# A fused attention and feed-forward kernel: 32-column matmuls written to the four row quarters of a PSUM bank

## The chip, the cores and the metric

The kernel runs on one core of one Trainium2 chip. The metric is the device time of one execution in microseconds (us), less is better. The core's engines are TensorE (PE; its weight loads are listed apart as PEld), VectorE (DVE), ScalarE (ACT), GpSimd (POOL) and SyncE (SP, which here issues all DMAs). Each engine works its own instructions off in order and waits for others by semaphores.

## The reference

An attention through 32 inducing points, then a feed-forward block whose activation is a rational function, over 4 batches of 12480 rows of 128 numbers:

```python
def mab(q, kv):
    s = scale * (q @ kv.transpose(0, 2, 1))
    s = s - s.max(-1, keepdims=True)
    a = np.exp(s)
    a /= a.sum(-1, keepdims=True) + 1e-09
    return a @ kv
h = mab(I, x)            # 32 inducing rows attend to all 12480 rows: "pooling"
y = mab(x, h)            # every row attends to the 32 pooled rows

h1 = y @ w_in            # 128 -> 2048
P = a[0] + a[1] * h1 + a[2] * h1**2 + a[3] * h1**3
Q = 1.0 + abs(b[0]) * abs(h1) + abs(b[1]) * h1**2
out = (P / (Q + 1e-06)) @ w_out      # 2048 -> 128
```

## The kernel before, in words

Rows of x are taken in blocks of 480 (4 chunks of 120), 26 blocks a batch. The main work is the feed-forward block. A unit is one block and two of the sixteen 128-column pieces of w_in; there are 4 x 26 x 8 = 832 units, and `fast_ticks` (line 887) advances by one unit a step. In a step PE computes h of the next unit (`first`, tiles hp, f16), adds a shift (`moved`, hp from by and same) and multiplies the unit of 13 steps ago by w_out (`second`, two fp32 matmuls of 128x128 by 128x480 into po); DVE makes the instructions u<-hp, l<-u,all,hp and l<-l,all,u, ACT takes Abs, a logarithm and a sigmoid, POOL two instructions every second step.

Beside it, the attention of the batches is worked off by two generators, `ahead` (the pooling of the next batch) and `attend` (the rows' own attention). They yield what their next piece needs ("pe", "v" for DVE, "wait") with a cost; `side` (line 782) adds a gain a step to each account (`SPARE`, line 195: 0.75 for "pe", kept up to 2.5, at most 1.7 spent in a step) and lets a generator go on as far as the account covers. So the yields' costs set how the side work is spread over the steps. All of it is written in program order on each engine.

Two pieces of `ahead` concern us:

- `pass1` (line 372), the scores of the inducing points. Four blocks make a group; 26 blocks are six groups of four and one of two. Tile pc holds 128 rows, 32 for each of the four blocks. The stationary operand is a 128-column window of ind, which is 224 columns wide, zero but for the 32 inducing points in its middle, so that block j adds to rows 32 j to 32 j + 31 and adds zero elsewhere; the group's matmuls accumulate into one bank. DVE then copies pc to e and takes the maxima. Each matmul yields 0.8 (line 384).
- `pooled` (line 444), the weighted sums. After Exp on ACT, PE transposes a group of e (tile pt), ACT copies it to eT, and 16 matmuls (4 blocks j, 4 chunks c) of 120x32 by 120x129 all accumulate into rows 0 to 31 of tile ph (line 485); the 129th column of x is one and sums the weights. Each yields 0.2. DVE adds ph to the accumulator acc (32 rows). At the end of the batch acc gives rs and H, and HT is H transposed.

The operands come by DMA: x_c blocks as tiles xTa (pass1) and x_t blocks as tiles x (pooled), in four buffers each; the next block's load is written when the one before is taken, and POOL sets the column of ones of x. Batch 0's pass1 and pooled run before the main work, in `before` (line 976), with loads of four or three blocks at a time (xTw, xw), while the loads of the weights (raw) are slipped in between; DVE and POOL then convert the weights from 64-bit floats (cv), and `main` starts.

One PSUM bank, misc, is shared by all side matmuls (`misc`, line 218).

Of the kernel before, what the change touches and what calls it, by code (L numbers as in the profile page):

```python
# [9 lines left out]
F32 = mybir.dt.float32  # L10
# [6 lines left out]
ALU = mybir.AluOpType  # L17
PSUM = bass.MemoryType.PSUM

P = 128  # L20
TP = 120
M = 32
C = 128
HB = 4
BT = HB * TP
# [167 lines left out]
class Kernel:  # L193
# [78 lines left out]

    def setup(self):
        nc, cp = self.nc, self.cp
        self.ind = cp.tile([C, 7 * M], F32, name="ind")
        nc.vector.memset(self.ind, 0.0)
        nc.sync.dma_start(out=self.ind[:, 3 * M:4 * M], in_=self.ind_c)
        self.ident = cp.tile([P, P], F32, name="ident")
        make_identity(self.tc.nc, self.ident)
        self.ones = cp.tile([1, 4], F32, name="ones")  # L280
        nc.vector.memset(self.ones, 1.0)
        self.ident4 = cp.tile([M, 4, M], F32, name="ident4")
        for j in range(4):
            nc.vector.tensor_copy(out=self.ident4[:, j], in_=self.ident[0:M, 0:M])
        self.many = cp.tile([M, 4], F32, name="many")
        nc.vector.memset(self.many, 1.0)
        self.w_max = cp.tile([C, 8], F32, name="w_max")
        self.w_in = cp.tile([C, self.F], F32, name="w_in")
        self.w_out = cp.tile([P, self.NF, C], F32, name="w_out")
# [82 lines left out]
    def pass1(self, b):  # L372

        nc, ap = self.nc, self.ap
        X = mybir.AxisListType.X
        e = ap.tile([P, self.NG, BT], F32, tag="e", name=f"e{b}")
        mxs = ap.tile([P, self.NG, 2], F32, tag="mxs", name=f"mxs{b}")
        nc.gpsimd.memset(mxs, -3.0e38)
        xs = self.wide_columns(b) if self.boot else self.cols.pop((b, "a"))
        for g in range(self.NG):  # L380
            nb = min(4, self.NB - 4 * g)
            yield from self.landed("a", b, g)
            for j in range(nb):
                yield "pe", 0.8
                if j == 0:
                    pc = self.misc(f"pc{b}_{g}")
                nc.tensor.matmul(pc[:, 0:BT], self.ind[:, M * (3 - j):M * (7 - j)], next(xs), start=(j == 0), stop=(j == nb - 1))
            rows = slice(0, M * nb)
            for i in range(2):
                yield "v", 0.36  # L390
                c = slice(BT // 2 * i, BT // 2 * (i + 1))
                nc.vector.tensor_scalar(out=e[rows, g, c], in0=pc[rows, c], scalar1=1.0, scalar2=None, op0=ALU.mult, op1=ALU.max, accum_out=mxs[rows, g, i:i + 1])
            self.free()
        if self.boot:
            self.wide_rows(b)
        else:
            self.xs[b] = [self.x_rows(b, n) for n in range(4)]
        yield "v", 0.1
        mx = ap.tile([P, 1], F32, tag="mx", name=f"mx{b}")
        nc.vector.tensor_reduce(out=mx, in_=mxs.rearrange("p g i -> p (g i)"), axis=X, op=ALU.max)  # L400
        yield "pe", 0.2
        pm = self.misc(f"pm{b}")
        nc.tensor.transpose(out=pm[0:1, 0:P], in_=mx, identity=self.ident)
        yield "v", 0.3
        mt = ap.tile([1, 1, M], F32, tag="mt", name=f"mt{b}")
        nc.vector.tensor_reduce(out=mt[:, 0], in_=pm[0:1, 0:P].rearrange("o (j m) -> o m j", m=M), axis=X, op=ALU.max)
        self.free()
        nm = ap.tile([1, 4, M], F32, tag="H", name=f"nm{b}")
        nc.vector.tensor_scalar(out=nm, in0=mt.broadcast_to((1, 4, M)), scalar1=-1.0 / math.sqrt(C), scalar2=None, op0=ALU.mult)
        yield "pe", 0.2  # L410
        pb = self.misc(f"pb{b}")
        nc.tensor.matmul(pb[:, 0:4], nm.rearrange("o j m -> o (j m)"), self.ones, start=True, stop=True)
        yield "v", 0.1
        nmc = ap.tile([P, 1], F32, tag="nmc", name=f"nmc{b}")
        nc.vector.tensor_copy(out=nmc, in_=pb[:, 0:1])
        self.free()
        self.e[b] = e
        self.exps.append(lambda: self.exp_rows(b, e, nmc))
        self.flush()
# [24 lines left out]
    def pooled(self, b, own=None):  # L444

        nc, ap = self.nc, self.ap
        e = self.e[b]
        acc = ap.tile([M, C + 1], F32, tag="acc", name=f"acc{b}")
        xs = self.xs.pop(b)

        def turned(g):
            rows = slice(0, M * min(4, self.NB - 4 * g))
            for c in range(HB):
                yield "pe", 0.22
                if c == 0:
                    pt = self.misc(f"pt{b}_{g}").rearrange("p (c n) -> p c n", c=HB)
                nc.tensor.transpose(out=pt[0:TP, c, rows], in_=e[rows, g, TP * c:TP * c + TP], identity=self.ident[rows, rows])
            eT = ap.tile([TP, HB, P], F32, tag="eT", name=f"eT{b}_{g}", bufs=2)
            yield from self.act(lambda: nc.scalar.activation(eT[:, :, rows], pt[0:TP, :, rows], AF.Identity, bias=0.0, scale=1.0))
            eTs.append(eT)  # L460

        eTs, early = [], int(self.boot)
        while self.e_done.get(b, 0) < self.NG:
            self.flush()
            yield "wait", 0
        if early:
            yield from turned(0)
        for g in range(self.NG):
            nb = min(4, self.NB - 4 * g)
            if g + early < self.NG:  # L470
                yield from turned(g + early)
            eT = eTs.pop(0)
            self.free()
            yield from self.landed("x", b, g)
            for k in range(HB * nb):
                j, c = divmod(k, HB)
                yield "pe", 0.2
                if k == 0:
                    ph = self.misc(f"ph{b}_{g}")
                if c == 0 and self.boot and (4 * g + j) % 3 == 0 and g + j:  # L480
                    self.xs[b] = xs
                    self.wide_rows(b)
                elif c == 0 and not self.boot and 0 < 4 * g + j < self.NB - 3:
                    xs.append(self.x_rows(b, 4 * g + j + 3))
                nc.tensor.matmul(ph[0:M, 0:C + 1], eT[:, c, M * j:M * j + M], xs[4 * g + j][:, c, :], start=(k == 0), stop=(k == HB * nb - 1))
            yield "v", 0.2
            if g == 0:
                nc.vector.tensor_copy(out=acc, in_=ph[0:M, 0:C + 1])
            else:
                nc.vector.tensor_tensor(out=acc, in0=ph[0:M, 0:C + 1], in1=acc, op=ALU.add)  # L490
            self.free()
        yield "v", 0.2
        rs = ap.tile([M, 1], F32, tag="rs", name=f"rs{b}")
        nc.vector.tensor_scalar(out=rs, in0=acc[:, C:], scalar1=1e-9, scalar2=None, op0=ALU.add)
        nc.vector.reciprocal(out=rs, in_=rs)
        yield "v", 0.2
        H = ap.tile([M, C], F32, tag="H", name=f"H{b}")
        nc.vector.tensor_scalar(out=H, in0=acc[:, 0:C], scalar1=rs, scalar2=None, op0=ALU.mult)
        yield "pe", 0.3
        pt = self.misc(f"HT{b}")  # L500
        nc.tensor.matmul(pt[:, 0:4 * M], H, self.ident4.rearrange("p a m -> p (a m)"), start=True, stop=True)
        yield "v", 0.2
        while own is None and self.scored < b - 2:
            yield "wait", 0
        HT = own if own is not None else ap.tile([C, 4 * M], F32, tag="HT", name=f"HT{b}", bufs=2)
        nc.vector.tensor_copy(out=HT, in_=pt[:, 0:4 * M])
        self.free()
        self.HT[b] = HT
# [436 lines left out]
    def last_on_pool(self, d, before):  # L945

        G, p = self.nc.gpsimd, self.params
        if d:
            G.tensor_scalar(out=before.u, in0=d.g, scalar1=1.0, scalar2=p.z_k3, op0=ALU.mult, op1=ALU.add)
            G.tensor_tensor(out=d.g, in0=before.u, in1=d.u, op=ALU.mult)  # L950
# [25 lines left out]
    def before(self):  # L976

        nc = self.nc
# [4 lines left out]
        self.setup()  # L983
        loads, words = self.weights(), []
        for n, _ in enumerate(self.pass1(0)):
            if n >= 36 and n % 6 == 3:
                words += [w for w in [next(loads, None)] if w]
        self.params = Params(self.tc.nc, self.cp, self.moe_a, self.moe_b)
        for n, _ in enumerate(self.pooled(0, self.cp.tile([C, 4 * M], F32, name="HT0"))):
            if n % 20 == 5:  # L990
                words += [w for w in [next(loads, None)] if w]
        words += list(loads)
        self.params.derive()
# [106 lines left out]
```

## Time and profile before

| what | value |
|---|---|
| time, median of 3 runs | 2593.8 us (2586.8 to 2594.12) |
| the profiled execution, its own time | 2591.88 us |
| its span, first to last instruction | 2589.7 us |
| mean granted TensorE clock | 0.974 |
| busy: PE, DVE, ACT, POOL | 92%, 88%, 83%, 56% of the span |

How to read it: a busy share is an average over the whole span; the main work begins some 115 us into it, and from about 1800 us on `ahead` has nothing left to do. What a piece of work costs is read from stretches of equal numbers of steps. Matmul records overlap in the trace (a record's length holds its latency), so the pace is taken from starts, not lengths. An fp32 matmul shows as two weight loads and two matmul records. All instructions of the main work bear line 177, that of a helper; they are told apart by their tiles.

### The profile page before, as it was taken

Reading aid. Unit: us, or ns where it says so; the run is one execution under the profiler, and the core shown is the slowest. Engines: PE = TensorE matmul, PEld = TensorE weight load, DVE = VectorE, ACT = ScalarE, POOL = GpSimd, SP = SyncE. Lnnn points to the kernel's source line nnn. Section 1 sums busy time; section 2 is a strip of 40 time slices with the busy share of each in tenths; the row PEclk is TensorE's granted clock in tenths of the full one; section 3 lists DMA queues with packets and bytes.
Section 4 is the critical chain, followed back from the end, with each engine's and each line's share of the span. In section 5 each row is a group of like instructions: output and inputs, shape, how many; then the busy total and the mean of one; then the engine's idle time right before and its main releaser. Section 6 shows DMA issues by size and latency. Waiting matters only on the chain.

```text
span 2589.7 us, 25944 instructions
## 1 busy us (share of the span) xinstructions
PE 2376.2 (92%) x8662; PEld 1206.7 (47%) x8662; DVE 2267.1 (88%) x2487; ACT 2151.0 (83%) x1487; POOL 1448.1 (56%) x997
## 2 busy tenths in 40 slices
PE   8589998999989999899999999999999999999997
PEld 5344544455544444455544444554444444444443
DVE  2698899878998899888899889888999999999996
ACT  1178789978887889988888789887889899899996
POOL 0335456555655565555655555555656566666666
PEclk9679999999999999999999999999999999999999
DMA  9112210021011310121121210221010101000000
GB/s 241 60 31 72 83 52 12 27 69 50 27 54 53 88 54 16 35 62 50 31 62 54 81 40 25 62 58 38 20 45 18 44 16 33 14 23 20 16 16 17
DMA packets 117112, 121.03 MB, mean 47 GB/s; under 512 B 13289, under 2 KB 115561, under 8 KB 116969
## 3 DMA queue, kind: packets, MB, share of 16 engines
q1 hardware_dynamic: 116969, 119.28, 16.3%
q8 instruction: 70, 1.15, 0.2%
q14 instruction: 73, 0.60, 0.1%
HBM read 80.89 MB, written 25.56 MB: 41 GB/s over the span
## 4 chain that ended last, share of the span: by engine, by line
PE 50%; DVE 28%; issue 8%; ACT 7%; POOL 2%; DMA 1%; SPq 1%; DVEq 0%; POOLq 0%; ACTq 0%
PE po L177 29%; DVE l L177 12%; DVE u L177 11%; PE hp L177 11%; ACT u L177 5%; PE pd L177 3%; PE ph L177 3%; PE pc L177 2%; DVE oT L177 1%; ACT L177 1%; POOL l L177 1%; DVE asm L177 1%; POOL u L177 1%; SPq L177 1%; PE pl L177 1%
## 5 line engine op out<-in xcount | busy, mean ns | idle before, releaser
L177 PE MATMUL po<-l,w_out 128*128 128x480 f32 x3328 | 1568.2, 575 | 10.6 <-POOL l L177 8.4
L177 DVE SCALAR_TENSOR_TENSOR l<-u,all,hp 128x960 f32<-128x960 f32 x832 | 1001.8, 1204 | 44.8 <-PE hp L177 29.9
L177 POOL TENSOR_SCALAR u<-l,all 128x960 f32<-128x960 f32 x416 | 446.2, 1073 | 945.6 <-DVE l L177 796.5
L177 POOL TENSOR_TENSOR l<-u 128x960 f32<-128x960 f32 x416 | 927.7, 2230 | 34.6
L177 PEld LDWEIGHTS po<-l,w_out 128*128 128x128 f32 x3328 | 624.3, 192 | 372.3 <-issue 209.2
L177 ACT ACTIVATE u<-u,all 128x1920 f32<-128x1920 f32 x416 | 765.6, 1887 | 1.2
L177 ACT ACTIVATE u<-u 128x1920 f32<-128x1920 f32 x416 | 737.5, 1797 | 3.0 <-DVE l L177 1.8
L177 DVE TENSOR_SCALAR u<-hp 128x960 int32<-128x960 int32 x520 | 597.2, 1148 | 125.1 <-PE hp L177 118.3
L177 ACT ACTIVATE u<-hp,all 128x960 f32<-128x960 f32 x312 | 328.2, 1052 | 289.8 <-PE hp L177 289.1
L177 DVE SCALAR_TENSOR_TENSOR l<-l,all,u 128x960 f32<-128x960 f32 x416 | 523.9, 1260 | 2.4 <-ACT u L177 2.4
L177 PE MATMUL hp<-at,st 128*128 128x480 f16 x1664 | 477.5, 369 | 20.4 <-DVE l L177 17.9
L177 PE MATMUL hp<-same,by 96*128 96x480 f16 x1040 | 301.3, 371 | 129.9 <-DVE u L177 124.6
L177 PEld LDWEIGHTS <-st 128*128 128x128 f16 x1872 | 182.6, 98 | 483.8 <-issue 468.7
L177 ACT ACT_TABLE_LOAD x235 | 301.5, 1283 | 4.7 <-PEq L1093 0.7
L177 PEld LDWEIGHTS <-by 96*128 96x128 f16 x1040 | 102.3, 98 | 356.7 <-issue 319.4
L177 DVE COPY oT<-po 128x480 f32<-128x480 f32 x104 | 67.8, 652 | 68.9 <-PE po L177 68.4
L177 PEld LDWEIGHTS pd<-HT,xTb 128*120 128x120 f32 x832 | 104.9, 200 | 16.4 <-issue 8.9
L177 PE MATMUL pd<-HT,xTb 128*120 128x32 f32 x832 | 101.8, 278 | 2.9 <-DMA xTb<-x_c 2.6
L177 PE MATMUL ph<-x,eT 120*32 120x129 f32 x624 | 76.7, 274 | 1.6 <-DMA x<-x_t 1.6
L177 PEld LDWEIGHTS ph<-x,eT 120*32 120x32 f32 x624 | 65.0, 109 | 22.6 <-issue 14.8
L177 PE MATMUL pc<-xTa,ind 128*128 128x480 f32 x156 | 71.9, 566 | 1.0 <-DMA xTa<-x_c 1.0
L177 PE MATMUL po<-at,st 128*128 128x480 f16 x208 | 59.1, 366 | 0.0
(108 smaller groups left out, 666.9 us busy)
## 6 DMA issues: line engine op xcount, KB each, us to landing
xTb<-x_c SPq DMA_DIRECT2D x104, 240.0 KB, 2.8
out<-oT SPq DMA_DIRECT2D x104, 240.0 KB, 2.0
xTa<-x_c SPq DMA_DIRECT2D x78, 240.0 KB, 2.7
x<-x_t SPq DMA_DIRECT2D x78, 240.0 KB, 3.4
at<-hl SPq DMA_DIRECT2D x416, 30.0 KB, 1.8
xw<-x_t SPq DMA_DIRECT2D x8, 720.0 KB, 13.6
xTw<-x_c SPq DMA_DIRECT2D x5, 960.0 KB, 11.9
raw<-w_in SPq DMA_DIRECT2D x4, 480.0 KB, 12.3
```

What stands on the lines that cost most here:

```text
L177: ins = call(*args, **kw)
```

## The change

Both kinds of matmul use a 32-column stationary operand and write 32 rows of the bank at a quarter's offset. In `pass1` ind is the inducing points alone, and block j of a group writes rows 32 j to 32 j + 31 in a matmul of its own, with no accumulation. In `pooled` chunk c writes quarter c, accumulated over the blocks j, so ph and acc have 128 rows; a new constant fold (four identities of 32 under each other) sums the quarters by one matmul per batch (pq), from which rs and H are made. The yields become 1.0 for a group in pass1 and 0.4 for four matmuls in pooled, and the weights' loads in `before` are placed by other counts, since there are fewer yields.

```diff
-        self.ind = cp.tile([C, 7 * M], F32, name="ind")
-        nc.vector.memset(self.ind, 0.0)
-        nc.sync.dma_start(out=self.ind[:, 3 * M:4 * M], in_=self.ind_c)
+        self.ind = cp.tile([C, M], F32, name="ind")
+        nc.sync.dma_start(out=self.ind, in_=self.ind_c)
...
+        self.fold = cp.tile([P, M], F32, name="fold")
+        for j in range(4):
+            rows = slice(M * j, M * j + M)
+            nc.vector.tensor_copy(out=self.fold[rows], in_=self.ident[rows, rows])
...
+            yield "pe", 1.0
+            pc = self.misc(f"pc{b}_{g}")
             for j in range(nb):
-                yield "pe", 0.8
-                if j == 0:
-                    pc = self.misc(f"pc{b}_{g}")
-                nc.tensor.matmul(pc[:, 0:BT], self.ind[:, M * (3 - j):M * (7 - j)], next(xs), start=(j == 0), stop=(j == nb - 1))
+                nc.tensor.matmul(pc[M * j:M * j + M, 0:BT], self.ind, next(xs), start=True, stop=True)
...
-        acc = ap.tile([M, C + 1], F32, tag="acc", name=f"acc{b}")
+        acc = ap.tile([P, C + 1], F32, tag="acc", name=f"acc{b}")
...
-                yield "pe", 0.2
+                if c == 0:
+                    yield "pe", 0.4
...
-                nc.tensor.matmul(ph[0:M, 0:C + 1], eT[:, c, M * j:M * j + M], xs[4 * g + j][:, c, :], start=(k == 0), stop=(k == HB * nb - 1))
+                nc.tensor.matmul(ph[M * c:M * c + M, 0:C + 1], eT[:, c, M * j:M * j + M], xs[4 * g + j][:, c, :], start=(j == 0), stop=(j == nb - 1))
             yield "v", 0.2
             if g == 0:
-                nc.vector.tensor_copy(out=acc, in_=ph[0:M, 0:C + 1])
+                nc.vector.tensor_copy(out=acc, in_=ph[:, 0:C + 1])
             else:
-                nc.vector.tensor_tensor(out=acc, in0=ph[0:M, 0:C + 1], in1=acc, op=ALU.add)
+                nc.vector.tensor_tensor(out=acc, in0=ph[:, 0:C + 1], in1=acc, op=ALU.add)
             self.free()
-        yield "v", 0.2
+        yield "pe", 0.3
+        pq = self.misc(f"pq{b}")
+        nc.tensor.matmul(pq[0:M, 0:C + 1], self.fold, acc, start=True, stop=True)
+        yield "v", 0.4
...
-        nc.vector.tensor_scalar(out=H, in0=acc[:, 0:C], scalar1=rs, scalar2=None, op0=ALU.mult)
+        nc.vector.tensor_scalar(out=H, in0=pq[0:M, 0:C], scalar1=rs, scalar2=None, op0=ALU.mult)
+        self.free()
...
-            if n >= 36 and n % 6 == 3:
+            if n >= 18 and n % 3 == 1:
...
-            if n % 20 == 5:
+            if n % 8 == 5:
```

The change also moves instructions, since the yields' costs set the places. On PE, the second group of batch 1's scores (pc_1; po, hp are the main work, st and by its f16 weights, xTa_n the blocks of x), before:

```order
L177 MATMUL pc_1_1274<-xTa_4_1198,ind 128x480
L177 MATMUL pc_1_1274<-xTa_5_1229,ind 128x480
L177 MATMUL po_2_0_1245<-l_2_3_1040,w_out 128x480
L177 LDWEIGHTS st_612
L177 MATMUL hp_4_2_1282<-at_1_0_1110,st_612 128x480
L177 LDWEIGHTS st_612
L177 MATMUL hp_4_2_1282<-at_1_0_1110,st_612 128x480
L177 MATMUL po_2_0_1245<-l_2_3_1040,w_out 128x480
L177 MATMUL pc_1_1274<-xTa_6_1242,ind 128x480
```

and now:

```order
L177 MATMUL hp_4_0_1256<-same,by 128x480
L177 MATMUL pc_1_1280<-xTa_4_1204,ind 32x480
L177 MATMUL pc_1_1280<-xTa_5_1207,ind 32x480
L177 MATMUL pc_1_1280<-xTa_6_1210,ind 32x480
L177 MATMUL pc_1_1280<-xTa_7_1281,ind 32x480
L177 MATMUL po_2_0_1252<-l_2_3_1046,w_out 128x480
```

A group of four stood on three steps (its fourth matmul follows one step later) and stands on one; over batches 1 to 3 the 78 pc matmuls stood on 54 steps and stand on 21, often two steps apart.

On PE, the first group of batch 1's pooling (ph_0; "x4" is one block's four chunks), the second half of it before:

```order
L177 MATMUL po_14_0_2820<-l_14_6_2711,w_out 128x480
L177 LDWEIGHTS by
L177 MATMUL hp_16_4_2880<-same,by 128x480
L177 MATMUL ph_0_2891<-x_2_2021,eT_0_2768 32x129 x4
L177 MATMUL ph_0_2891<-x_3_2024,eT_0_2768 32x129 x4
L177 MATMUL po_14_0_2820<-l_14_7_2721,w_out 128x480
```

and the whole group now:

```order
L177 MATMUL hp_12_6_2466<-same,by 128x480
L177 MATMUL ph_0_2496<-x_0_1569,eT_0_2452 32x129 x4
L177 MATMUL ph_0_2496<-x_1_1572,eT_0_2452 32x129 x4
L177 MATMUL ph_0_2496<-x_2_1575,eT_0_2452 32x129 x4
L177 MATMUL ph_0_2496<-x_3_1578,eT_0_2452 32x129 x4
L177 MATMUL po_11_0_2522<-l_11_0_2286,w_out 128x480 x2
```

The two halves of a group stood on two steps that follow each other (13 steps a batch, 39 in all) and now stand on one (7 a batch, 21 in all), the next group five or more steps later. The group stands some 30 steps earlier in the program than before.

On DVE, at the end of batch 0's pooling, before the main work (acc takes up the last group, ph_6; cv are the conversions of the weights), now:

```order
L177 SCALAR_TENSOR_TENSOR cv_515<-raw_180,cv_515 128x480
L177 TENSOR_TENSOR acc_214<-ph_6_392,acc_214 128x129
L77 TENSOR_TENSOR all<-all 128x1
L177 TENSOR_SCALAR cv_523<-raw_189 128x480
L146 CAST flag<-all 128x1
L177 TENSOR_SCALAR rs_406<-pq_404 32x1
```

The last accumulation stands inside the first of the eleven conversions (cv_515); before, it stood behind four whole ones and the start of two more.

## Rows read from the trace of the kernel before

**Rows 1.** The page: span, engines' busy time, POOL's two groups of the main work.

```profile
span 2589.7 us, 25944 instructions
PE 2376.2 (92%) x8662; PEld 1206.7 (47%) x8662; DVE 2267.1 (88%) x2487; ACT 2151.0 (83%) x1487; POOL 1448.1 (56%) x997
...
L177 POOL TENSOR_SCALAR u<-l,all 128x960 f32<-128x960 f32 x416 | 446.2, 1073 | 945.6 <-DVE l L177 796.5
L177 POOL TENSOR_TENSOR l<-u 128x960 f32<-128x960 f32 x416 | 927.7, 2230 | 34.6
```

**Rows 2.** Busy time in three stretches of 16 steps: scores, pooling, neither.

```profile
core 0: us, PE busy (x) PEld busy (x) DVE busy (x) ACT busy (x) POOL busy (x), PEclk, DMA share, GB/s
1439.20:1489.10 49.90, 47.95 (x147) 22.45 (x146) 45.25 (x54) 42.47 (x29) 27.34 (x17) 1.00 0.25 70
1630.50:1681.40 50.90, 49.07 (x213) 26.87 (x213) 41.39 (x43) 42.59 (x32) 28.93 (x26) 1.00 0.22 60
2396.40:2436.30 39.90, 37.77 (x121) 17.58 (x120) 39.55 (x38) 39.38 (x27) 26.37 (x16) 1.00 0.06 19
```

**Rows 3.** Groups of these three stretches: count, busy us, mean ns, idle us before.

```profile
L177 DVE SCALAR_TENSOR_TENSOR l<-u,all,hp 128x960 f32<-128x960 f32 x17 | 20.5, 1204 | 0.6 <-PE hp L177 0.6
L177 PE MATMUL pc<-xTa,ind 128*128 128x480 f32 x24 | 11.1, 565 | 0.0
...
L177 DVE SCALAR_TENSOR_TENSOR l<-u,all,hp 128x960 f32<-128x960 f32 x17 | 20.5, 1205 | 2.1 <-PE hp L177 2.0
L177 PE MATMUL ph<-x,eT 120*32 120x129 f32 x80 | 10.0, 274 | 0.6 <-DMA x<-x_t 0.6
...
L177 DVE SCALAR_TENSOR_TENSOR l<-u,all,hp 128x960 f32<-128x960 f32 x17 | 20.4, 1202 | 0.0
```

**Rows 4.** Groups of the whole span, by form: pc, ph and acc.

```profile
L177 PE MATMUL ph<-x,eT 120*32 120x129 f32 x624 | 76.7, 274 | 1.6 <-DMA x<-x_t 1.6
L177 PE MATMUL pc<-xTa,ind 128*128 128x480 f32 x156 | 71.9, 566 | 1.0 <-DMA xTa<-x_c 1.0
...
L177 DVE TENSOR_TENSOR acc<-ph,acc 32x129 f32<-32x129 f32 x24 | 6.7, 277 | 6.0 <-PE ph L177 6.0
```

**Rows 5.** PE in order of time around four pc records: start, length, what.

```profile
1445.01 1.77 PE L177 MATMUL pc<-xTa,ind 128*128 128x480 f32 x4
1446.62 0.97 PE L177 MATMUL po<-l,w_out 128*128 128x480 f32 x2
```

**Rows 6.** PE in order of time around a burst of ph.

```profile
593.81 0.57 PE L177 MATMUL hp<-at,st 128*128 128x480 f16 x2
594.22 0.97 PE L177 MATMUL po<-l,w_out 128*128 128x480 f32 x2
595.02 0.57 PE L177 MATMUL hp<-same,by 96*128 96x480 f16 x2
595.52 1.96 PE L177 MATMUL ph<-x,eT 120*32 120x129 f32 x16
597.41 1.07 PE L177 MATMUL po<-l,w_out 128*128 128x480 f32 x2
```

**Rows 7.** The weight loads of that burst and the next, idle time in brackets.

```profile
595.52 1.69 PEld L177 LDWEIGHTS ph<-x,eT 120*32 120x32 f32 x16 [0.40 <-issue]
597.41 0.30 PEld L177 LDWEIGHTS po<-l,w_out 128*128 128x128 f32 x2 [0.20 <-issue]
```

**Rows 8.** The page's DMA issues: count, KB each, us from issue to landing.

```profile
xTa<-x_c SPq DMA_DIRECT2D x78, 240.0 KB, 2.7
x<-x_t SPq DMA_DIRECT2D x78, 240.0 KB, 3.4
```

**Rows 9.** Busy time before the main work, in stretches; DMA share last but one.

```profile
8.00:16.00 8.00, 7.50 (x13) 3.45 (x14) 1.07 (x8) 0.00 (x0) 0.12 (x1) 1.00 1.02 428
16.00:60.00 44.00, 36.65 (x188) 25.44 (x186) 11.81 (x120) 6.49 (x10) 0.84 (x7) 0.88 1.10 204
60.00:71.00 11.00, 10.26 (x90) 9.28 (x88) 10.10 (x30) 0.98 (x2) 3.71 (x3) 1.00 1.03 300
71.00:95.00 24.00, 7.37 (x34) 6.97 (x34) 21.23 (x56) 0.00 (x0) 8.64 (x9) 0.58 0.16 48
```

**Rows 10.** DVE in order of time at the end of the conversions.

```profile
94.92 0.29 DVE L177 SCALAR_TENSOR_TENSOR w_out<-cv 128x128 f32<-128x128 int32 x1 [0.62 <-POOL cv L177]
95.65 0.69 DVE L177 TENSOR_REDUCE amx<-pd 120x16 f32<-120x512 f32 x1 [0.44 <-DVE w_out L177]
```

More of the change, by code (lines that the diff above doesn't have):

```diff
@@ L484, in pooled @@
                     xs.append(self.x_rows(b, 4 * g + j + 3))
-                nc.tensor.matmul(ph[0:M, 0:C + 1], eT[:, c, M * j:M * j + M], xs[4 * g + j][:, c, :], start=(k == 0), stop=(k == HB * nb - 1))
+                nc.tensor.matmul(ph[M * c:M * c + M, 0:C + 1], eT[:, c, M * j:M * j + M], xs[4 * g + j][:, c, :], start=(j == 0), stop=(j == nb - 1))
             yield "v", 0.2
             if g == 0:
-                nc.vector.tensor_copy(out=acc, in_=ph[0:M, 0:C + 1])
+                nc.vector.tensor_copy(out=acc, in_=ph[:, 0:C + 1])
             else:
-                nc.vector.tensor_tensor(out=acc, in0=ph[0:M, 0:C + 1], in1=acc, op=ALU.add)
+                nc.vector.tensor_tensor(out=acc, in0=ph[:, 0:C + 1], in1=acc, op=ALU.add)
             self.free()
-        yield "v", 0.2
+        yield "pe", 0.3
+        pq = self.misc(f"pq{b}")
+        nc.tensor.matmul(pq[0:M, 0:C + 1], self.fold, acc, start=True, stop=True)
+        yield "v", 0.4
         rs = ap.tile([M, 1], F32, tag="rs", name=f"rs{b}")
-        nc.vector.tensor_scalar(out=rs, in0=acc[:, C:], scalar1=1e-9, scalar2=None, op0=ALU.add)
+        nc.vector.tensor_scalar(out=rs, in0=pq[0:M, C:C + 1], scalar1=1e-9, scalar2=None, op0=ALU.add)
         nc.vector.reciprocal(out=rs, in_=rs)
```

## The prediction

> **What bounds the kernel now.** First I read the page: three engines are near full, PE 92%, DVE 88%, ACT 83% of a 2589.7 us span [rows 1], so no average says which of them sets the time. The kernel repeats one step 832 times (one DVE instruction l<-u,all,hp each), so I cut the span into stretches of 16 steps and asked each engine's busy time there [rows 2]. (By instructions they hold 17 each, 16 steps and one cut at an edge [rows 3].) Late in the program, with nothing but the main work left, 16 steps take 39.9 us, 2.49 us a step, with DVE and ACT busy for 39.55 and 39.38 us and PE for 37.77: DVE and ACT bound that stretch, and PE has 2.1 us to spare, 0.13 us a step. In a stretch with 24 pc records 16 steps take 49.9 us, and in one with 80 ph records 50.9 us; there PE is busy for 47.95 and 49.07 us while DVE falls to 45.25 and 41.39. So wherever the next batch's scores (pc) or its pooling (ph) run beside the main work, TensorE sets the pace, and those are the matmuls that the change touches. The clock plays no part: the granted clock is 1.00 in all three stretches, TensorE's upper level, 2.4 GHz.
>
> **What these matmuls cost now.** Each fp32 matmul is two records (78 pc matmuls in batches 1 to 3, 156 records; 312 ph matmuls, 624) [rows 4]. Four pc records stand 1.61 us ahead of the next po: 0.4025 us a record [rows 5]. Sixteen ph weight loads span 1.69 us [rows 7], 0.106 us each; the 274 ns that a record shows is its latency [rows 4]. A ph burst also pays at its edges. Of the records around one [rows 6], the two of hp before it start at 595.02 and stream for 0.40 us (the two at 593.81 stand 0.41 us ahead of the next record), so ph could start at 595.42 and starts at 595.52; 16 x 0.106 = 1.70 us later, at 597.22, po could start, and starts at 597.41, after 0.20 us in which no weights were loaded [rows 7]; and its first pair takes 1.07 us where the pair at 594.22 took 0.97. Together 0.10 + 0.19 + 0.10 = 0.39 us a burst. pc, which uses the same 128x128 shape as po, pays none of it.
>
> So on PE: pc 156 x 0.4025 = 62.8; ph 624 x 0.106 = 66.1; edges 39 bursts x 0.39 = 15.2: 144.1 us. By the order of the instructions this lies on 54 + 39 = 93 steps, each of which first fills the 0.13 us that PE has spare: 144.1 - 12.1 = **132.0 us of the time is these matmuls**. The stretches agree: 10.0 us extra for 24 records and 11.0 for 80 make 65 + 86 = 151, an upper bound, since other side work lies in both.
>
> **What the change makes of it.** Shape [128, 32] takes the place of [128, 128] in pc, and four matmuls to four quarters stand next to each other, 18 groups of four and 3 of two for pc, and for ph the same 21 groups with 16 or 8 matmuls, each group now in one step (before: pc over 2 to 4 steps, ph over 2). What a quad costs on PE no row shows. Bounds: all four wait for each other (0.4025 x 8 = 3.22 us a pc quad, as now), or all four run at once (0.805 us). I take a value between, from the rows: a matmul is two records and the second needs the same quarter as the first, so, if records start in program order, the second record of one matmul and the first of its neighbour can run together and nothing more. A pc quad is then 5 slots instead of 8, a pair 3 instead of 4; in a ph burst of 16 the chain goes on, 17 slots instead of 32, and 9 instead of 16 in a burst of 8.
> - pc: 18 x (5 x 0.4025 + 0.39) + 3 x (3 x 0.4025 + 0.39) = 43.2 + 4.8 = 48.0. The 0.39 is new here.
> - ph: 18 x (17 x 0.106 + 0.39) + 3 x (9 x 0.106 + 0.39) = 39.5 + 4.0 = 43.5. Half the bursts go, and their edges.
> - the fold matmul pq, once a batch: 3 x (2 x 0.106 + 0.39) = 1.8.
>
> Sum 93.3, less 42 steps x 0.13 = 5.5: 87.8. **Saved: 132.0 - 87.8 = 44 us.** PE remains the bound in these stretches: the other engines' own excess there is 5.7 us of DVE for 24 pc records (45.25 - 39.55) and 3.2 us of ACT for 80 ph records (42.59 - 39.38), 37 + 25 = 62 us in all, below 87.8.
>
> **The smaller edits.** The accumulator is 128 rows instead of 32 with the same 129 columns: the DVE form takes 0.28 us [rows 4] and works row beside row; I take 0, covered by PE in the ph stretches; without that cover its 28 instructions would be 7.8 us. H and rs read PSUM instead of SBUF, four times: 0, bounds -1 to +1.
>
> A new wait: the fourth operand of a group is fetched (and its ones column set by POOL) in the step whose burst uses it, where before it was used a step later. POOL is in order; every second step gives it 1.07 + 2.23 us of main work first [rows 1], and SP may hold an output store ahead of it. What PE waits for these operands now is 1.6 and 1.0 us in all [rows 4]; a load lands in 2.7 to 3.4 us [rows 8], and the last user of the buffer is two to five steps back, 5 us or more. I take +2, bounds 0 and +30 (18 groups, half of them behind 3.3 us of POOL).
>
> Before the main work: pass 1 of batch 0 gets cheaper on PE, but the DMA engines are full from 8 to 71 us [rows 9] and load the same bytes, and then DVE's weight conversion runs to 95.2 us [rows 10], the last thing that the first row work waits for. The new order sets ten of the eleven conversions behind the last accumulation. I take 0, bounds -5 and +5.
>
> The sum: 44 - 2 = 42 us. The profiled execution took 2591.9 us (2.2 outside its span), the median of the runs is 2593.8; the forecast is 2593.8 - 42 = **2552 us**. I call a change of 0.3%, 7.8 us, no change: about what a measurement of this kernel can tell.
>
> **Rivals.**
> *All four at once.* pc 18 x (0.805 + 0.39) + 3 x 1.195 = 25.1; ph 18 x (8 x 0.106 + 0.39) + 3 x (4 x 0.106 + 0.39) = 24.7; fold 1.8; less 5.5: 46.1. That is below the 62 us at which DVE and ACT take over, so 132 - 62 = 70 us are saved: 2593.8 - 70 + 2 = 2526. For it: the quads write different rows and need nothing of each other. Against it: the two records of a matmul. The Trainium skill ("TensorE: Matmul & The Clock Gate", Part 3, on packing small matmuls) says that matmuls to different 32-column tiles overlap almost wholly, a few ns apart, and gives 2.38 times for three of them: that is this rival. The same section says that matmuls start in program order without reordering, which with two records per matmul is the forecast. No row here shows either.
>
> *One after the other* (the change doesn't do what it says), and slower. pc 62.8 + 21 x 0.39 = 71.0; ph 66.1 + 21 x 0.39 = 74.3; fold 1.8; less 5.5 (the work sits on 42 steps instead of 93, and so uses less of PE's spare time): 141.6, 9.6 more than now, with the 2: 2605, 0.45% slower. It decides from the point at which overlap gives back less than 12 us of the 129 that the records take. For it: no stretch of this trace has two matmuls side by side.
>
> *The array drains at every change of quarter.* Half of the 0.39 us at each of 57 + 291 changes is 68 us on top of that: 2674. Against it: within a burst the stationary operand changes at every record and nothing is lost between records now [rows 7]; so I give it little. The Trainium skill ("TensorEngine Tiling (Array Packing)", Key Properties) says that a change of the tiling shape drains the engine and a change of tile alone does not; by that rule this case would not arise.
>
> *In between*: an overlap in ph alone or in part, or the new waits at their upper bound, within 7.8 us of now.
>
> **How the numbers follow.** Forecast 0.43, all at once 0.25, in between 0.09, one after the other 0.18, drains 0.05. Faster: 0.43 + 0.25 and 0.02 of the in-betweens, 0.70; same 0.07 + 0.02 of the serial case, 0.09; slower 0.16 + 0.05 = 0.21. The range is 2515 to 2606: the full overlap with some 10 us less of the other engines' excess (part of which is not of pc or ph), up to the serial case. It leaves out the drains and the tails, under 2 in 10. The forecast's own range, with the 0 to +30 of the waits and the -5 to +5 at the start, is 2540 to 2580.
>
> **What would show it.** In the changed profile the records of neighbouring pc matmuls should start one slot (0.40 us) apart in pairs, a quad taking about 2.0 us from its first record to the next po, and a ph burst of 16 about 1.8; at 0.8 and 0.9 the first rival holds, at 3.2 and 3.4 the second; more than that means drains. A stretch with pc should still show PE above 95% in the steps with a burst; where DVE or ACT reach 97% there, the gain has hit their floor. PE idle behind x or xTa by more than a few us means the new wait. The start of the main work should stay within 5 us of now. I am wrong if the time lies above 2586: then quads do not overlap, or what they give back is taken by waits.

## The result, and the profile after

The changed kernel takes 2563.8 us (median of 4 runs, 2559.11 to 2570.45) against 2592.07 for the kernel before in the same session: ratio 0.9896, 95% interval 0.9866 to 0.9925, by which it is 27 us less. That is inside the range and 12 us above the forecast of 2552. The experiments below show that two terms of the forecast were far off, in opposite directions.

| | before | after |
|---|---|---|
| profiled execution, us | 2591.9 | 2566.8 |
| span, us | 2589.7 | 2564.9 |
| first l<-u,all,hp at, us | 116.3 | 118.0 |
| mean granted clock | 0.974 | 0.956 |

The page of the kernel after, its span and the engines' busy time (against [rows 1]):

```profile
span 2564.9 us, 25969 instructions
PE 2285.1 (89%) x8670; PEld 1112.6 (43%) x8670; DVE 2269.3 (88%) x2490; ACT 2149.7 (84%) x1487; POOL 1445.7 (56%) x997
```

PE lost 91 us of busy time, DVE, ACT and POOL none. But part of PE's loss lies ahead of the main work, where nothing depends on it. So the main work alone, from the first l<-u,all,hp to the end, first the kernel before, then the one after (length, then busy time and count of PE, PEld, DVE, ACT, POOL, the granted clock, the DMA share):

```profile
116.30:2589.70 2473.40, 2300.49 (x8319) 1156.87 (x8317) 2215.84 (x2263) 2136.77 (x1464) 1427.58 (x954) 0.98 0.14 41
```

```profile
118.00:2564.90 2446.90, 2236.78 (x8325) 1087.65 (x8324) 2216.73 (x2263) 2135.49 (x1464) 1425.47 (x954) 0.97 0.14 41
```

PE is busy 63.7 us less, and idle 2446.9 - 2236.8 = 210.1 us where it was idle for 172.9: 37.2 us more. The difference, 26.5 us, is the gain. So the question is in two parts: what the quarters saved, and what made PE idle.

**What the quarters saved.** PE in order of time, a group of four pc matmuls (8 records) and a pooling group of 16 ph matmuls (32 records), both with all operands there (start, length, what; against [rows 5] and [rows 6]):

```profile
1215.27 0.57 PE L177 MATMUL hp<-at,st 128*128 128x480 f16 x2
1215.67 0.97 PE L177 MATMUL po<-l,w_out 128*128 128x480 f32 x2
1216.57 1.01 PE L177 MATMUL pc<-xTa,ind 128*32 128x480 f32 x8
1217.51 1.07 PE L177 MATMUL po<-l,w_out 128*128 128x480 f32 x2
1218.42 0.57 PE L177 MATMUL hp<-at,st 128*128 128x480 f16 x2
...
1505.34 0.57 PE L177 MATMUL hp<-same,by 96*128 96x480 f16 x2
1505.84 1.09 PE L177 MATMUL ph<-x,eT 120*32 120x129 f32 x32
1506.86 1.07 PE L177 MATMUL po<-l,w_out 128*128 128x480 f32 x2
1507.77 0.57 PE L177 MATMUL hp<-at,st 128*128 128x480 f16 x2
```

Eight pc records stand 0.94 us ahead of the next po, where four took 1.61; 32 ph records 1.02 us, where 16 took 1.89. The trace's single records show how. In this pc group the first records of the four matmuls start at 1216.568, 1216.574, 1216.581 and 1216.588 us, 7 ns apart, and their second records at 1216.994 to 1217.014: the quarters run at once, both records of each matmul. Here all first records start ahead of all second ones. In another group, whose fourth operand came late, the second records of three matmuls start at 231.175 to 231.188 us, before the first record of the fourth at 231.224. So the records follow neither the order of their matmuls nor one of all firsts and then all seconds. Narrower operands alone give nothing: two such matmuls that did not overlap took 1.89 us (e11 below), 0.94 each. With the edges counted as in the prediction (0.10 us before a burst, 0.10 in the pair behind it) a pc group costs 1.14 us and a ph group 1.22. The rival *all four at once* had 1.195 and 1.24, the forecast 2.40 and 2.19. The Trainium skill ("TensorE: Matmul & The Clock Gate", Part 3) says that matmuls on different 32-column tiles overlap a few ns apart; the trace agrees with its 7 ns, for fp32 matmuls of two records too.

The accumulation on 128 rows takes 291 ns, where it took 277 [rows 4], nearly what the prediction assumed:

```profile
L177 DVE TENSOR_TENSOR acc<-ph,acc 128x129 f32<-128x129 f32 x24 | 7.0, 291 | 31.2 <-PE ph L177 31.2
```

**What made PE idle.** PE's waits for the operands of these groups (total us, times, longest), which were 1.6 and 1.0 us in [rows 4]:

```profile
PE ph L177 <- DMA x<-x_t: 14.0, 3, 9.6
...
PE pc L177 <- DMA xTa<-x_c: 10.7, 2, 7.7
PE ph L177 <- POOL x L177: 10.0, 8, 2.3
```

That is 34.7 us. And a group whose fourth operand is late without stopping PE loses overlap all the same, since the last matmuls then run by themselves. The next group after the pc one above, again 8 records, and the po behind it:

```profile
1222.15 2.02 PE L177 MATMUL pc<-xTa,ind 128*32 128x480 f32 x8
1224.10 1.07 PE L177 MATMUL po<-l,w_out 128*128 128x480 f32 x2
```

It took 1.95 us, not 0.94. Of the 18 groups of four, seven of pc took 0.94 us and six of ph 1.02; the others took longer. All the while a load itself takes little longer than in [rows 8] (the page's DMA issues, last number us from issue to landing):

```profile
xTa<-x_c SPq DMA_DIRECT2D x78, 240.0 KB, 3.0
x<-x_t SPq DMA_DIRECT2D x78, 240.0 KB, 4.0
```

The longest stall, first what PE does, then SP's queue:

```profile
1519.20 0.87 PE L177 MATMUL ph<-x,eT 120*32 120x129 f32 x24
1529.64 0.66 PE L177 MATMUL ph<-x,eT 120*32 120x129 f32 x8 [9.57 <-DMA x<-x_t]
```

```profile
1519.87 0.37 SPq L177 DMA_DIRECT2D out<-oT  x1
1520.64 4.94 SPq L177 DMA_DIRECT2D at<-hl  x8
1525.69 1.58 SPq L177 DMA_DIRECT2D x<-x_t  x3
```

Twelve of the group's 16 matmuls are done in 0.87 us; the last four need the fourth operand, whose load stands in SP's queue behind an output store and eight at<-hl copies of 0.6 us each. It is issued at 1525.69, and lands 3.8 us later. The main work behind it on PE waits too. At 1238.30 the same happens to pc (7.74 us). The stretches around this stall:

```profile
1490.00:1520.10 30.10, 28.99 (x150) 14.07 (x150) 25.14 (x26) 25.84 (x19) 17.88 (x20) 0.94 0.23 59
1520.10:1529.60 9.50, 0.00 (x0) 0.00 (x0) 1.93 (x2) 0.56 (x1) 0.65 (x4) 0.73 0.39 112
1529.60:1534.60 5.00, 4.96 (x16) 2.35 (x17) 2.63 (x3) 3.29 (x3) 2.64 (x2) 0.50 0.16 35
1534.60:1540.00 5.40, 5.40 (x20) 2.48 (x19) 3.41 (x3) 2.26 (x3) 0.74 (x2) 0.99 0.00 0
```

and behind the one of pc:

```profile
1238.30:1241.10 2.80, 2.80 (x5) 0.61 (x6) 0.96 (x3) 0.00 (x0) 0.00 (x0) 0.50 0.53 171
```

The granted clock falls while PE idles, and for the 5.0 us behind the stall it is 0.50, the lower of its two levels (1.2 GHz), with PE busy all the time. So the stall costs its 9.5 us and half of these 5.0. Added up over the main work, the lower level was granted for 81 us before and 133 us after; PE was busy for 71 of the 81 and for 111 of the 133, and half of these 40 us more is 20. The Trainium skill (the same page, Terms) puts the loss at half the time on the lower level: an estimate of 26 us for the 52 more, an upper bound where PE was idle in part of it.

### The profile page after: what moved, and what is told of

It is laid out like the page before. It is cut to its first block, busy times and chain, and to the rows that moved or that the text cites. A ratio compares the mean times of both kernels' runs of the same rounds, so it can differ in the third digit from the quotient of the medians.

```text
span 2564.9 us, 25969 instructions
## 1 busy us (share of the span) xinstructions
PE 2285.1 (89%) x8670; PEld 1112.6 (43%) x8670; DVE 2269.3 (88%) x2490; ACT 2149.7 (84%) x1487; POOL 1445.7 (56%) x997
## 4 chain that ended last, share of the span: by engine, by line
PE 44%; DVE 33%; issue 11%; ACT 6%; DMA 3%; POOL 2%; SPq 1%; DVEq 0%; POOLq 0%; ACTq 0%
PE po L177 27%; DVE l L177 15%; DVE u L177 12%; PE hp L177 10%; ACT u L177 4%; PE pd L177 3%; DVE oT L177 2%; ACT L177 1%; DVE asm L177 1%; PE pc L177 1%; SPq L177 1%; POOL u L177 1%; DMA xw<-x_t 1%; DMA xTw<-x_c 1%; DVE cv L177 1%
## 5 line engine op out<-in xcount | busy, mean ns | idle before, releaser
L177 DVE TENSOR_SCALAR_CACHE_REDUCE e<-pc 128x240 f32<-128x240 f32 (+1 forms) x56 | 21.1, 401 | 31.9 <-PE pc L177 31.9
L177 ACT ACTIVATE a<-a 120x512 f32<-120x512 f32 (+2 forms) x21 | 14.9, 728 | 41.1 <-DVE a L177 41.0
L177 PE MATMUL ph<-x,eT 120*32 120x129 f32 x624 | 25.6, 292 | 24.0 <-DMA x<-x_t 14.0
## 6 DMA issues: line engine op xcount, KB each, us to landing
raw<-w_in SPq DMA_DIRECT2D x4, 480.0 KB, 10.3
```

The lines of the kernel that those rows point to most:

```text
L177: ins = call(*args, **kw)
```

## The experiments

All medians, ratios to the kernel before on the same chip in the same session, with 95% intervals. Idle is PE's wait behind x, xTa and POOL's column of ones together (before: 2.6).

| run | what | us | ratio | idle, us |
|---|---|---|---|---|
| after | quarters, yields and loads of the change | 2563.8 | 0.9896 [0.9866, 0.9925] | 34.7 |
| e1 | after + early loads | 2516.5 | 0.9710 [0.9685, 0.9734] | 0.2 |
| e2 | quarters in the scores alone | 2582.4 | 0.9966 [0.9949, 0.9982] | 6.6 |
| e3 | quarters in the pooling alone | 2556.8 | 0.9876 [0.9856, 0.9896] | 22.2 |
| e4 | yields alone, no quarters | 2622.8 | 1.0123 [1.0102, 1.0144] | 17.4 |
| e5 | e4 + early loads | 2593.1 | 1.0020 [1.0004, 1.0035] | 0 |
| e6 | before + early loads | 2586.6 | 0.9982 [0.9970, 0.9994] | 0 |
| e7 | after + early loads of x | 2535.3 | 0.9793 [0.9773, 0.9813] | 10.5 |
| e8 | e2 + early loads of xTa | 2563.1 | 0.9894 [0.9877, 0.9911] | 0.5 |
| e9 | e1, batch 0's scores as before | 2522.3 | 0.9728 [0.9707, 0.9749] | 0 |
| e10 | e3 + early loads of x | 2534.0 | 0.9780 [0.9760, 0.9800] | 0 |
| e11 | after in the yields of before | 2567.9 | 0.9907 [0.9887, 0.9928] | 6.8 |
| e12 | e1 with half pooling bursts | 2539.9 | 0.9795 [0.9769, 0.9821] | 0 |

**e1, early loads: the late operand alone.** The next group's four loads go out behind a group's last matmul, in place of one by one a group's matmuls ahead:

```diff
+            if not self.boot:
+                self.ready_a += [self.x_columns(b, n, "a") for n in range(4 * g + 4, min(4 * g + 8, self.NB))]
...
-                elif c == 0 and not self.boot and 0 < 4 * g + j < self.NB - 3:
-                    xs.append(self.x_rows(b, 4 * g + j + 3))
...
+            if not self.boot:
+                xs += [self.x_rows(b, n) for n in range(4 * g + 4, min(4 * g + 8, self.NB))]
```

> The changed kernel, but the four operands of the next group (xTa in pass1, x in pooled) are all loaded, and the ones column of x set, in the step in which the group before ended, instead of the fourth one in the step whose burst uses it. Theory A (the lost part of the gain is PE waiting for the fourth operand, whose load stands behind an output store and eight copies in SP's queue): PE's idle behind xTa, x and POOL's x, 10.7 + 14.0 + 10.0 us in the changed kernel, falls below 6 us, and the time to about 2535 us (2525 to 2545), with fewer stretches at half clock. Theory B (the bursts empty TensorE so that its clock falls to half, 97 us of the main work against 49 before, and that costs the gain): the waits go but the half-clock stretches stay, and the time stays within 2550 to 2562. Theory C (DVE and ACT are the bound once the quads overlap): no change, 2556 to 2566.

Measured: 2516.5 us, 47 below after and 74 below before, more than any theory gave it. (The 97 and 49 us at half clock that the expectation names are less than the 133 and 81 that the whole main work adds up to.) The waits are gone; below, all that is left of them in PE's list, and then the main work in one row, as above:

```profile
PE pc L177 <- DMA xTa<-x_c: 0.2, 1, 0.2
```

```profile
122.90:2515.40 2392.50, 2213.17 (x8325) 1080.20 (x8324) 2210.06 (x2263) 2133.16 (x1463) 1425.30 (x954) 0.98 0.15 42
```

Against after PE is idle 30.8 us less (179.3 for 210.1), and busy 23.6 us less for the same 8325 instructions. By the trace's records 10.3 of these lie in the pc and ph groups themselves, which no longer wait for a fourth matmul (17 of 18 now take 0.94 and 17 of 18 take 1.02 us), and 13.2 outside of them: there PE was busy at the lower clock for 77 us in place of 105, and half of that difference is 14. So the late operand cost its idle time, some 10 us of lost overlap and some 13 of the clock. The last is the roughest: in e9 and e12, which have no such waits either, PE was busy at the lower clock for 15 and 7 us more than in e1. Theory B, that the clock falls without the stalls and keeps the time above 2550, and C, that DVE and ACT are the floor, fall. The same view of e1: the first stretch holds 16 steps with 24 pc records, the second 16 steps with 96 ph records:

```profile
794.30:840.10 45.80, 42.94 (x148) 18.57 (x147) 43.38 (x53) 41.23 (x29) 27.42 (x17) 0.96 0.26 81
1439.20:1482.40 43.20, 42.19 (x229) 21.05 (x228) 41.48 (x44) 41.76 (x31) 28.20 (x30) 1.00 0.29 72
```

They took 49.9 (24 pc) and 50.9 us (80 ph) before [rows 2]. PE, DVE and ACT are now at 94, 95 and 90% in the first, at 98, 96 and 97% in the second: no engine is the bound by itself any more.

**e4 and e5: the same yields without overlap.** e4 is after with the matmuls of before (zero-padded columns in pc, one row quarter in ph, no fold); e5 adds e1's edit.

```diff
-                nc.tensor.matmul(pc[M * j:M * j + M, 0:BT], self.ind, next(xs), start=True, stop=True)
+                nc.tensor.matmul(pc[:, 0:BT], self.ind[:, M * (3 - j):M * (7 - j)], next(xs), start=(j == 0), stop=(j == nb - 1))
...
-                nc.tensor.matmul(ph[M * c:M * c + M, 0:C + 1], eT[:, c, M * j:M * j + M], xs[4 * g + j][:, c, :], start=(j == 0), stop=(j == nb - 1))
+                nc.tensor.matmul(ph[0:M, 0:C + 1], eT[:, c, M * j:M * j + M], xs[4 * g + j][:, c, :], start=(k == 0), stop=(k == HB * nb - 1))
```

> The matmuls of the kernel before (128 columns with accumulation, rows 0 to 31), but the changed yields and load places: a whole group in one step. If the gain is the overlap of the quads, this has none: 2592 + 10 for the spare time lost on fewer steps + 20 to 35 for the late operands, 2605 to 2640. If the gain came from the planner's yields, it stays near 2564.

> The matmuls of the kernel before (32 zero-padded columns of one shape for pc, one row quarter for ph, no fold), issued in the yields of the changed kernel, with the early loads of e1_early_loads: nothing overlaps and no operand is late, so e1 (2516.5) against this run is the price of the overlap by itself, and one_yields_alone (e4, 2622.8) against it the price of the late operand without overlap. Theory A (the late operand costs what e1 showed, 47 us, with or without overlap): 2622.8 - 47 = 2576, range 2566 to 2588, and the overlap is worth 60 us. Theory P (the prediction's sum for one after the other: 9.6 us more than before on PE, nothing else): 2592 + 10 = 2602, range 2594 to 2610, and the overlap is worth 85 us, near the 95 us of PE time that the sum gives it (141.6 - 46.1). PE idle behind x and xTa under 2 us in both.

Measured: e4 2622.8, as expected, and e5 2593.1. In e5's main work, as above:

```profile
115.60:2584.80 2469.20, 2295.88 (x8319) 1160.30 (x8319) 2211.44 (x2263) 2134.75 (x1463) 1426.59 (x954) 0.98 0.14 41
```

From e5 to e1 nothing changes but the quarters, the narrower ind and the fold: PE is busy 82.7 us less, and the main work is 76.7 us shorter. So **overlap is worth 77 us** (80 by the ratios, since the two ran on different chips), and PE was the bound for nearly all of it. And the late operand costs 30 us without overlap (e4 to e5; 27 by the ratios) against 47 with it, with PE idle for 17.4 and 34.7 us. The likely reason, which no run tests by itself: a group of four that runs for 3.2 us hides more of a late load than one of 0.94. Theory A of e5, which had 47 for both, falls. The time of e5 lies 0.9 us below the range of theory P; but P's 9.6 us hold 8.2 for the edges of pc, which e5, whose pc has the shape of po, does not pay, so this run does not test that term.

**e6: early loads on the kernel before**, e1's edit there.

> The kernel before, with only the early loads of e1 (the four loads of the next group behind a group's last matmul). Theory A (early loads are worth only what PE waited for operands): PE was idle 1.6 us behind x and 1.0 us behind xTa there, so 2587 to 2594, no change. Rival C (the place of the loads helps in itself, by SP's queue or the DMA engines, so that part of e1's 47 us is no wait of the change): 2575 or less. Rival D (four loads at once come in the way of the weight copies and stores): above 2597.

Measured: ratio 0.9982, 3 to 5 us, within 0.3%. So the early loads are worth at most 5 us by themselves; the rest of the 47 us is a cost that the change brought.

**e7: early loads of x alone**, the second and third piece of e1's edit.

> The changed kernel with early loads for the pooling (x) only; xTa keeps its place. Theory A by the idle time of the trace of after: 14.0 us behind x and 10.0 behind POOL for x against 10.7 behind xTa, so two thirds of e1's 47 us come with this edit: 2532, range 2525 to 2542, PE idle behind x under 1 us, behind xTa still 6 to 12. Rival: the stalls behind xTa cost more than their idle time (the weight loads of the main work wait as well): 2543 to 2556.

Measured: 2535.3, within A's range, with PE still idle 10.5 us behind xTa. 28.5 us come from the pooling's loads, 18.8 from the scores': 18.8 us for 10.5 us of idle time. The rival's time is missed, but that these stalls cost more than their idle time holds.

**e2, e3, e8, e10: one half at a time.** e2 has the change in the scores alone, e3 in the pooling alone; e8 and e10 give each its early loads.

> Only the scores (pass1) are written to quarters; pooled is that of the kernel before. If quads overlap as the changed trace shows, PE saves 62.8 - 25 = 38 us and loses about 11 to xTa: A expects 2568 (2562 to 2576), 15 to 30 us under the kernel before. B expects more half clock in the stages with pc and 2580 or more.

> Only the pooling (pooled, with fold) is written to quarters; pass1 is that of the kernel before. PE saves 81 - 27 = 54 us and loses about 24 to x (DMA and POOL): A expects 2570 (2562 to 2580). With e2 the two savings should add up to the 28 us of the whole, within 10.

> e2 (the quarters in the scores alone, pooling as before; 2582.4) with early loads of xTa. Theory A (e2 fell short of its 2562 to 2576 by the late xTa: 6.6 us of PE idle there, 11.8 of weight loads): 2562 to 2574. Rival E (the score quads are worth little, because DVE has 45.3 us of work in 16 such steps and takes over): 2577 to 2584, no better than e2.

> e3 (the quarters and the fold in the pooling alone, scores as before; 2556.8) with early loads of x. Theory A (e3 still holds a late x, 18.3 us of PE idle behind x and 3.9 behind POOL, and e7 got 28 us back for 24 such us): 2531, range 2523 to 2540; then the two halves with early loads, -27 (e8) and -59, make more than e1's -73, as the halves without them (-8 and -34) made more than the whole's -28, and the 13 us are no matter of the loads. Rival F (the halves add up once no operand is late, and the missing 13 us were the loads): -73 + 27 = -46, 2543, range 2540 to 2548.

Measured: e2 2582.4, 6 us above A's range and within B's, with 6.6 us of idle time behind xTa; but the lower clock, which B blames, was granted for 77 us of its main work, no more than before (81), and early loads mend it (e8). e3 is 2556.8, 5 us below its range and no worse than the whole change (their intervals overlap), though it has 22.2 us of idle time itself. With early loads e8 is 2563.1 (19 better) and e10 2534.0 (23 better), in the ranges of theory A both; E and F miss them. By the ratios the halves without early loads give 9 + 32 = 41 us where the whole gives 27; with them 27 + 57 = 84 where e1 gives 75. The intervals of three ratios add up to some 10 us, so the first difference, 14 us, stands just clear of them, and the second, 9 us, may be none. What makes the halves worth more than the whole is not shown, nor whether the loads have a part in it.

**e9: batch 0's scores as before**, for the start of the main work.

```diff
+                if self.boot:
+                    nc.tensor.matmul(pc[:, 0:BT], self.ind[:, M * (3 - j):M * (7 - j)], next(xs), start=(j == 0), stop=(j == nb - 1))
+                else:
+                    nc.tensor.matmul(pc[M * j:M * j + M, 0:BT], self.ind[:, 3 * M:4 * M], next(xs), start=True, stop=True)
```

> e1 (2516.5) with the score matmuls of batch 0 alone, before the main work, as in the kernel before (zero-padded columns, one after the other); quarters in all later batches. In the traces so far the first l<-u,all,hp starts at 118.0, 122.9, 120.7, 118.1 and 121.8 us where batch 0's scores are in quarters, at 116.3, 116.7, 115.6, 112.6 and 115.2 where they are not. Theory S (the quarters cost the start some 5 us): first step at 113 to 117, time 2508 to 2514. Rival (spread of the runs, nothing of the edit): 2514 to 2520, first step 118 or later.

Measured: 2522.3, its interval overlapping e1's, with the first step at 118.6 us (118.6 in e10 too, whose scores there are also as before). Theory S misses on both its numbers: nothing was gained. But that the quarters leave the start alone is not shown. Over all profiled executions the first step comes at 112.6 to 118.6 us in the seven kernels with batch 0's scores as before, and at 118.0 to 122.9 in the seven with quarters there (119.5 in e11, 122.0 in e12), some 4 us apart on average.

**e11: the change in the yields of before**, so that an operand is used a step or more after its load is issued.

```diff
-            yield "pe", 1.0
-            pc = self.misc(f"pc{b}_{g}")
             for j in range(nb):
+                yield "pe", 0.8
+                if j == 0:
+                    pc = self.misc(f"pc{b}_{g}")
...
-                if c == 0:
-                    yield "pe", 0.4
+                yield "pe", 0.2
```

> The changed matmuls (quarters and fold) in the yields and load places of the kernel before: a group's four scores again over 2 to 4 steps, a pooling group over 2 steps of 8 matmuls, each operand used a step or more after its load is issued. Theory A (after lost to the late fourth operand, and quarters overlap wherever they stand next to each other): the waits are gone without early loads, PE idle behind x and xTa under 3 us in all; pc overlaps in the steps with two, 54 steps x 0.94 = 51, ph 39 bursts x 0.6 = 23, with the fold and 93 steps x 0.13 to spare 64 us of PE against 132: 68 us less, at the floor of 62 that DVE and ACT set, so 2592 - 62 = 2530, range 2518 to 2545. Rival B (the waits come from the shorter PE work itself, which leaves every load less time, whatever the yields): idle 8 us or more behind x and xTa, 2550 to 2570.

Measured: 2567.9, 23 us above A's range and within that of rival B. The waits are mostly gone (6.8 us for 34.7; 9.3 with one of 2.5 us for ph that PE's list puts to POOL's u), though not under A's 3 us, and still the time is that of after. Two pairs of the scores, 4 records each, and then a stall that has nothing to do with the edit:

```profile
805.38 1.00 PE L177 MATMUL pc<-xTa,ind 128*32 128x480 f32 x4
806.31 1.07 PE L177 MATMUL po<-l,w_out 128*128 128x480 f32 x2
...
809.34 1.96 PE L177 MATMUL pc<-xTa,ind 128*32 128x480 f32 x4
811.23 0.58 PE L177 MATMUL hp<-at,st 128*128 128x480 f16 x2
```

```profile
119.50:2569.30 2449.80, 2265.65 (x8325) 1086.48 (x8324) 2212.43 (x2263) 2135.53 (x1464) 1426.62 (x954) 0.98 0.14 41
...
825.00:833.50 8.50, 8.50 (x47) 5.30 (x45) 8.50 (x9) 8.33 (x6) 5.51 (x3) 1.00 0.09 33
833.50:839.90 6.40, 0.12 (x2) 0.05 (x1) 2.36 (x3) 4.08 (x3) 3.28 (x2) 0.69 0.40 117
839.90:846.10 6.20, 6.20 (x14) 3.55 (x15) 0.69 (x1) 0.00 (x0) 0.00 (x0) 0.50 0.37 115
846.10:850.90 4.80, 4.80 (x16) 2.20 (x15) 3.94 (x5) 1.93 (x2) 0.00 (x0) 1.00 0.00 0
```

A pair takes as long (0.93 us) as a group of four in one step (0.94), and where its second operand is late, 1.89. PE is busy 52.5 us more than in e1, and the time is 51 us longer. By the records, 33 of these 52.5 us lie in the pc and ph groups themselves, now in 53 and 39 pieces in place of 21 and 21: 75 us in all where e1 has 42, and A's sum had 51 + 23. Outside of them PE was busy at the lower clock for 26 us more, and half of that is 13; that and the remaining 6 were not in A's sum, which also held the other engines' floor of 62 us to be what is left to gain. At 833.5 PE stands idle for 6.3 us behind a load of xTb, which is not of these groups but of the attention's next part, again with a row of 0.59 us copies ahead of it in SP's queue, and runs at 0.50 for the 6.2 us that follow. The waits behind xTb come to 18.8 us in this run, to 3.8 in after: A had taken the waits of other loads as fixed. That shorter PE work leaves every load less time, B's reason, would fit this wait, but 18.8 us in one run do not show it.

**e12: e1 with half bursts**, the `yield "pe", 0.2` of the last diff, and the weights' loads in `before` counted by it.

> e1 (2516.5) with each pooling group's 16 matmuls in two steps of 8, as in the kernel before, in place of one step. Theory A (with no operand late, only the sum counts: 18 more bursts at some 0.2 of edge each, less 18 steps x 0.13 that PE has to spare): 2516 to 2522. Rival G (a 1.02 us burst in one step delays DVE and ACT there, and two half bursts hide better): 2500 to 2511.

Measured: 2539.9, slower than either theory; the single runs go from 2525.8 to 2540.8, and the profiled one, at 2525.8, shows 9.4 us more PE busy time than e1, about 4 of them by the clock, and nothing else that stands out. Both theories fall. Half bursts don't help; why three of the other four runs lie 14 us above the profiled one is open.

## Why the prediction was right, and where it was not

The sign, the range and the bound were right: TensorE sets the pace where this work lies beside the main work, and from e5 to e1 the main work got shorter by nearly what PE got back (76.7 of 82.7 us). The edges were right too: the rival's 1.195 and 1.24 us, with the same 0.39 in each, met 1.14 and 1.22. The accumulation on 128 rows and the reads of PSUM cost nothing that can be seen, as assumed. The start was inside its 5 us in this kernel (the conversions end 1.9 us later, the first step comes 1.7 us later), though not in e1, where the first step comes 6.6 us later.

Two steps failed.
- **The price of a quad.** "The second record of one matmul and the first of its neighbour can run together and nothing more" is wrong, and so is its condition that records start in program order: all four quarters run at once, both records of each. With operands in time (e1) PE is busy 87 us less than before; the forecast had 144.1 - 93.3 = 51, the rival 144.1 - 51.6 = 92. In time that is 74 us against the forecast's 44.
- **The new wait.** "I take +2, bounds 0 and +30" is wrong in value and in its upper bound: 34.7 us of idle time and 47 us of time. The text named POOL, which has 10 of the 34.7, and one output store ahead of the load on SP; it missed the eight at<-hl copies, 4.94 us of SP's queue, in whose shadow the two long stalls lie. And it missed that a late operand takes its matmul out of the overlap (some 10 us), that it costs more with overlap (47 us) than without (30), and that the clock falls behind a stall: "the clock plays no part" held in the three stretches shown, and not in the changed kernel.

-74 and +47 make -27, as measured; the forecast had -44 and +2. That it came within 12 us is luck: both errors, 30 and 45 us, leaned against each other.

The rival *all four at once*, at 2526, had the mechanism and the edges right and shared the error on the wait: e1, which has no wait, is at 2516.5. Its floor of 62 us (DVE and ACT taking over, 70 us saved at most) is passed by a few us. *One after the other* and *drains* did not occur.

## What to carry to other kernels

Matmuls that fill one quarter of the array's columns are worth setting side by side, but only when all their operands are there: packing makes four operands due at once, so move their loads a group ahead with the matmuls. Look through the whole queue that issues these loads (here SP, with eight copies of 0.6 us) for what can stand ahead of them in the step, and price a late operand at its idle time, the lost overlap and the half-speed stretch behind it. Spread over several steps, the same quarters gained 24 us in place of 75 (e11, whose loads were not the early ones).

## What the runs showed of the hardware that was not expected

- fp32 matmuls to four 32-column quarters overlap, although each is two records: 0.94 us for eight records of 480 columns (3.22 us one after the other in e5), 1.02 us for 32 of 129 columns (3.66 in e5).
- The second record of a matmul can start before the first record of the next one or behind it: behind it by 406 ns where the operands were there (1216.588 and 1216.994 us), before it by 36 ns where one was late (231.188 and 231.224).
- Stalls of TensorE of 9.6, 7.7 and 6.3 us were followed by 5.0, 2.8 and 6.2 us in which PE, busy all the time, was granted the lower clock (0.50).
